# Scores of chunks 3 to 5 on 64x64 tiles of TensorE, four heads a matmul

## The chip, the cores and the metric

The kernel runs on one core of a Trainium2 chip. The metric is the device time of one execution in microseconds (us), as the median of several runs. TensorE (PE in the profile, with PEld for its weight loads) multiplies matrices, VectorE (DVE), ScalarE (ACT) and GpSimd (POOL) work elementwise, and SyncE (SP) issues nearly all DMAs.

## What is computed

The reference is a state-space attention block (Mamba-2, SSD) followed by an MLP with hard-swish. `x` is 4 batches x 8 heads x 768 tokens x 32, `B` and `C` have a state size of 16, and `a` is a decay of each token.

```python
log_a = np.log(np.clip(a, 1e-06, 1.0))
for c in range(nc):                                   # chunks of the sequence
    cum = np.cumsum(la, axis=-1)
    L = np.exp(cum[:, :, :, None] - cum[:, :, None, :]) * causal
    CB = np.einsum('bhin,bhjn->bhij', Cc, Bc)         # the scores
    y_intra = np.einsum('bhij,bhjd->bhid', CB * L, xc)
    y_inter = np.einsum('bhin,bhnd->bhid', Cc, state) * np.exp(cum)[:, :, :, None]
    y[:, :, sl] = y_intra + y_inter
    state = decay_full[:, :, None, None] * state + np.sum(Bx, axis=2)
# heads side by side: 3072 tokens x 256
h = x @ w_in                                          # 256 -> 2048
g = h * np.clip(h + 3.0, 0.0, 6.0) / 6.0
return (g @ w_out).astype(np.float32)                 # 2048 -> 256
```

The result of the recurrence does not depend on the chunk's length; the kernel uses chunks of its own.

## The kernel before

The kernel cuts the 768 tokens into `NC` = 6 chunks of 128, each split into two halves of 64 tokens. Chunk by chunk it does the attention part for all 4 batches and 8 heads, and then the MLP for the 512 tokens (4 batches x 128) of that chunk. The order of instructions is written out by hand: the attention work of chunk c = k + 1 is woven into the MLP of block k, and each engine takes its instructions in that order.

**One MLP block.** For k >= 1, the loop `for f in range(2, NF)` (L1084) is the first product, with 16 slices of 128 hidden units. Slice f's result `h` lies in one of six banks of PSUM (f0 to f3, y0, y1, in turn). `squares` (L696) starts the slice f, `cross` (L713) ends slice f - 2, `enlarge` (L704) scales the bank between them (on VectorE where f % 4 is 3, else on ScalarE), and `factor` does ramp and product of hard-swish: ScalarE writes `gT` from `h` (L730), VectorE multiplies it by `h` in place (L735). GpSimd makes sums of `gT` (`g_sums`, L784, its operations at L796) for the second product, at f = 6, 10, 14 and after the loop. Then `wide_units` (L865), a generator of 14 units, does the second product (matmuls at L874). It collects the output in two tiles, `wide` and `back`: VectorE transposes `wide` into `back` in blocks of 32x32 (`turned_back`, L882), and SP stores `back` in 32 DMAs of 16 KB. The last block has `out_units` (L798) in its place. In block 0, `first_out` (L738) writes the output through the same two buffers.

**The scores.** For chunk c, `bTs[c]` holds three tiles with state sizes and heads on the partitions (8 heads x 16 = 128) and tokens along the free dimension: `bT` from B, `csT` from C, and `cT`, two copies of C's transpose. Copy t of `cT` is zero except for the heads whose number is t modulo 2; `parity` (128x2) holds the zeros and ones for it. `scores` (L516) makes, for each batch b, half a and pair of heads q, one matmul on a tile of 32 rows x 64 columns: the 32 partitions of the pair from `bT` against those of both copies of `cT`, 2 x 64 = 128 columns, into the bank f{q}. That is 32 matmuls a chunk. `multiply` (L562) then multiplies the decays `L` by the scores on VectorE, one operation for each bank (L574), and `mix` (L604) multiplies the result by x.

**Where that stands.** The transposes of chunk `ahead` = k + 2 are made by `turn_all` (L483): for chunk 2 at the end of block 1's first product, for chunks 3 to 5 in unit 9 of block k's second product (L1141), on VectorE: two 32x32 transposes (L465), the two copies of `cT` (`part_heads`, L475) and `fade` (L481), which multiplies `csT` in place by decays for the products with the state. The scores of chunk c = 3, 4, 5 stand behind unit 2 of the second product of block k = c - 1 (L1124). For chunks 3 and 4, `own_banks` (L508) puts the products with the state (`from_state`, L503, tiles of 32x64) directly ahead of the scores; for chunk 5 they come one unit earlier (L1122). `into_state` (L544, tiles of 64x32) follows the scores.

`TURN` is 2. Chunks 0 and 1 are transposed in other ways, and chunk 2's copies are made on ScalarE.

Of the kernel before, what the change touches and what calls it, by code (L numbers as in the profile page):

```python
# [21 lines left out]
def kernel(  # L22
# [24 lines left out]
    nc = tc.nc  # L47
# [107 lines left out]
    def conceal_in(t, pattern):  # L155
# [27 lines left out]
        out=head, in_=head, pattern=[[2 * N, NQ], [N, 2]], compare_op=ALU.is_ge,  # L183
        fill=0.0, base=N - 1, channel_multiplier=-1)
    parity = const.tile([P, 2], FP32, name="parity")

    def decode(i):

# [211 lines left out]
    def carry(c):  # L400
# [3 lines left out]
            out=tmps[c], in0=states[c - 1],  # L404
            in1=etos[c][:, :, HT - 1:HT].to_broadcast([P, NB, 2 * D]), op=ALU.mult)

    def turned(c):
        if c not in bTs:
            bTs[c] = [att.tile([P, NB, P], FP32, name="bT", bufs=1),
                      att.tile([P, NB, 2, P], FP32, name="cT", bufs=1),  # L410
                      att.tile([P, NB, P], FP32, name="csT", bufs=1)]
        return bTs[c]

# [49 lines left out]
    def turn_squares(t, out):  # L463
# [2 lines left out]
            out=out.rearrange("r b (s a) -> r b a s", a=4),  # L466
            in_=t.rearrange("s t b a n -> s (b a) t n"))

    def part_heads(c):
        _, cT, csT = turned(c)  # L470
        for t in range(2):
            if c == TURN:
                nc.scalar.activation(cT[:, :, t], csT, AF.Copy, scale=parity[:, t:t + 1])
            else:
                nc.vector.tensor_scalar(  # L475
                    out=cT[:, :, t], in0=csT, scalar1=parity[:, t:t + 1], scalar2=None,
                    op0=ALU.mult)
# [5 lines left out]
    def turn_all(c):  # L483
        bT, _, csT = turned(c)
        for t, out_ in zip(bcs[c], (csT, bT)):
            turn_squares(t, out_)
        part_heads(c)
        fade(c)

    def busy(n, bank):  # L490

# [24 lines left out]
    def scores(c):  # L516

        bT, cT, _ = bTs[c]
        cbs[c] = [ps.tile([P, NB, 2, HT], FP32, name="cb", tag=f"f{q}") for q in range(NQ)]
        if c not in ys:
            own_banks(c)
        for b in range(NB):
            for a, rows in enumerate(HALF):
                for q in range(NQ):
                    pair = slice(32 * q, 32 * q + 32)
                    nc.tensor.matmul(  # L530
                        out=cbs[c][q][rows, b], lhsT=bT[pair, b, rows],
                        rhs=cT[pair, b, :, rows], start=(b == 0), stop=True,
                        tile_position=(32 * q, a * HT), skip_group_check=True)
        if c == TURN:
            from_state(c, 0)
        into_state(c, *range(2 if c not in (TURN, NC - 1) else 1))
# [25 lines left out]
    def multiply(c):  # L562

        if c < NC - 1 and c != TURN:
            take(c)
        mids[c] = mid = att.tile([P, NB, 2 * D], FP32, name="mid", bufs=1)
        if c == 0:
            for t in range(2):
                nc.scalar.activation(
                    mid[:, :, t * D:(t + 1) * D], sps[c][0][:, :, t * D:(t + 1) * D], AF.Copy,  # L570
                    scale=parity[:, t:t + 1])
        for q in (2, 0, 1, 3) if c in (TURN, NC - 1) else range(NQ):
            hs = slice(2 * q, 2 * q + 2)
            nc.vector.tensor_tensor(  # L574
                out=Ls[c][:, :, hs], in0=Ls[c][:, :, hs], in1=cbs[c][q], op=ALU.mult)
            if c and c != TURN and q == 1:
                new_state(mid, sps[c][0], tmps[c])

# [137 lines left out]
    def factor(k, f):  # L716
        ramp(k, f, hs_[k, f])
        times_ramp(k, f, hs_[k, f])
# [19 lines left out]
    def first_out(b, i, c):  # L738

        if i == 0 and b % 2 == 0:
            outs[b // 2] = ps_o.tile([P, 2, DM], FP32, name="o", tag="o")
        o = outs[b // 2]
        for f in range(i * FP, (i + 1) * FP):
            if b == NB - 1 and f >= NF - 2:
                lead(c, f - NF + 2)
            nc.tensor.matmul(  # L748
                out=o[:, b % 2], lhsT=gTs[0][:, f, b * P:(b + 1) * P], rhs=w_out[:, f],
                start=(f == 0 and b % 2 == 0), stop=True, skip_group_check=True)  # L750
        if i == NP - 1 and b % 2:
            ob = ffn.tile([P, 4, DM], FP32, name="ob", tag=("wide", "back")[b // 2])[:, :2]
            nc.scalar.copy(out=ob, in_=o)
            nc.sync.dma_start(
                out=out.rearrange("(b s) m -> s b m", b=NB)[:P, b - 1:b + 1], in_=ob)
# [42 lines left out]
    def out_units(k):  # L798


        def quarter(e, r, t):
            return g_quarter(k, e, r)[:, :, t * P:(t + 1) * P]

        def total(n, t):
            return gsums[k][n][:, :, t * P:(t + 1) * P]

        def unit(bank, slot, lhs, rhs, js=range(NJ), clear=False):

            for j in js:
                nc.tensor.matmul(  # L810
                    out=bank[:, slot], lhsT=lhs[:, j], rhs=rhs[:, j],
                    start=(clear and j == 0), stop=True, skip_group_check=True)

        for t in range(2):
            oa = ps_o.tile([P, 4, P], FP32, name="oa", tag="o")
            if t == 0:

                most, rest = range(NJ - 1), range(NJ - 1, NJ)
                unit(oa, 0, quarter(0, 0, 0), w4[:, 0, 0], most, clear=True)
                yield  # L820
                unit(oa, 3, quarter(0, 0, 1), w4[:, 0, 0], most)
                yield
            unit(oa, 1, quarter(1, 0, t), w4[:, 1, 0], clear=(t == 1))
            if t == 0:
                unit(oa, 0, quarter(0, 0, 0), w4[:, 0, 0], rest)
                unit(oa, 3, quarter(0, 0, 1), w4[:, 0, 0], rest)
                x1 = ffn.tile([P, 2, P], FP32, name="x1", tag="third")
                nc.scalar.copy(out=x1, in_=oa[:, 0:4:3])
            yield
            ob = ps_o.tile([P, 4, P], FP32, name="ob", tag="o")  # L830
            unit(ob, 3 - 3 * t, quarter(1, 1, t), wsums[4], clear=True)
            yield
            unit(oa, 2, total(2, t), wsums[2])
            res = ffn.tile([P, 8, P], FP32, name="res", tag=("wide", "back")[t])
            nc.vector.tensor_tensor(
                out=res[:, 0:5:4], in0=oa[:, 1:3],
                in1=x1[:, t:t + 1].to_broadcast([P, 2, P]), op=ALU.add)
            yield
            unit(ob, 2, total(4, t), w4[:, 1, 1])
            yield  # L840
            unit(ob, 3 * t, total(1, t), wsums[1])
            u = ffn.tile([P, 2, P], FP32, name="u", tag="u2")
            u2 = res[:, 4:5].to_broadcast([P, 2, P])
            if t:
                nc.vector.tensor_tensor(out=u, in0=ob[:, 0:4:3], in1=u2, op=ALU.add)
                nc.vector.tensor_tensor(out=res[:, 1], in0=ob[:, 2], in1=u[:, 1], op=ALU.add)
            yield
            if t:

                unit(oa, 0, quarter(0, 1, t), wsums[3], clear=True)  # L850
                nc.vector.tensor_tensor(
                    out=res[:, 2:4], in0=oa[:, 0:1].to_broadcast([P, 2, P]), in1=u, op=ALU.add)
            else:
                unit(ob, 1, quarter(0, 1, t), wsums[3])
                nc.vector.tensor_tensor(out=u, in0=ob[:, 0:2], in1=u2, op=ALU.add)
                nc.vector.tensor_tensor(out=res[:, 1:3], in0=ob[:, 2:4], in1=u, op=ALU.add)
                nc.vector.tensor_tensor(out=res[:, 3], in0=ob[:, 0], in1=u[:, 1], op=ALU.add)
            for r in range(2):
                r0 = (t + 2 * r) * S + k * P
                nc.sync.dma_start(  # L860
                    out=out[r0:r0 + P, :],
                    in_=res[:, 2 * r:2 * r + 2].rearrange("p m c -> p (m c)"))
            yield

    def wide_units(k):  # L865
# [10 lines left out]
                    start=(clear and j == 0), stop=True, skip_group_check=True)  # L876

        near, far = range(NJ // 2), range(NJ // 2, NJ)
        res = ffn.tile([P, 2, 2, 2 * P], FP32, name="wide")
        back = ffn.tile([P, 2, TB], FP32, name="back")  # L880

        def turned_back(m, r=None):  # L882

# [27 lines left out]
        yield  # L911
        product(oc, 0, w4[:, 1, 0], halves[1][0], far)
        product(oa, 0, w4[:, 0, 0], halves[0][0], far[-1:])
        nc.scalar.copy(out=res[:, 0, 0], in_=oc[:, 0])
        nc.vector.tensor_tensor(out=res[:, 0, 0], in0=oa[:, 0], in1=res[:, 0, 0], op=ALU.add)
        yield
# [103 lines left out]
    load_eto(1)  # L1020
    load_bc(1)
    load_x(1)


    weave, g_done = {}, {}
# [4 lines left out]
    for k in range(NC):  # L1030
# [53 lines left out]
        for f in range(2, NF):  # L1084
# [7 lines left out]
            cross(k, f - 2)  # L1092
            enlarge(k, f)
            factor(k, f - 2)
            if f in ((8, 12) if k == 1 else (3, 7)) and ahead < NC:
                conceal(ahead, int(f in (7, 12)))
            if f == NF - 1 and k not in gsums:
# [78 lines left out]
```

## Time and profile before

| | |
|---|---|
| median of 3 runs | 343.59 us (343.59 to 344.37) |
| the profiled execution | 343.4 us, of which the span of its instructions is 341.7 |
| TensorE busy | 333.8 us, 3372 matmul records |
| VectorE, ScalarE, GpSimd busy | 210.7, 188.3, 145.4 us |
| scores, L530 | 384 records, 7.4 us busy, a record 277 ns on average |
| copies of cT on VectorE, L475 | 8 operations, 4.2 us |
| granted clock of TensorE | 1.00 |

The profile shows one execution. A row names the line, the engine, the operation and the tiles it writes and reads, with the number of instructions, their busy time and the mean of one. Matmul records overlap each other, so the busy time of a group is less than the number times the mean. The chain of waits follows the work that ended last back to the start: what stands in it set the time. The time of a run is that of the whole launch and is a little longer than the span.

### The profile page before, as it was taken

What the parts mean: (1) busy time and instruction counts of PE and PEld (TensorE: products, weight loads), DVE (VectorE), ACT (ScalarE), POOL (GpSimd) and SP (SyncE); (2) the same over time, 40 slices, a digit from 0 to 9 for tenths busy, and PEclk for the clock granted to TensorE, in tenths of its full rate; (3) what the DMA queues carried; (4) which work ended last, traced back from release to release, by engine and by line L of the source; (5) the groups of instructions that cost most, each with busy time, mean ns of one, the idle gap of its engine ahead of it and who ended that gap; (6) DMA issues with size and microseconds to landing.
All of it is one profiled execution on the core that took longest, in us unless ns stands there. A gap on an engine that the chain in (4) does not pass through costs nothing.

```text
span 341.7 us, 8203 instructions
## 1 busy us (share of the span) xinstructions
PE 333.8 (98%) x3372; PEld 267.5 (78%) x3372; DVE 210.7 (62%) x332; ACT 188.3 (55%) x394; POOL 145.4 (43%) x139
## 2 busy tenths in 40 slices
PE   5999999999999999999999999999999999999996
PEld 2554448888878888888888888888888888888996
DVE  6699999996499739665519465528465323465011
ACT  4778878667987481675471676470576030576000
POOL 3300000381282998099803089810089600079600
PEclk9999999999999999999999999999999999999999
DMA  8989967052690216167107294001260001110000
GB/s 172 174 312 197 209 233 153 2 59 69 164 114 8 58 55 119 25 84 70 24 27 144 33 96 62 16 2 18 33 75 2 2 4 17 30 17 2 0 33 31
DMA packets 89605, 25.15 MB, mean 74 GB/s; under 512 B 82208, under 2 KB 85952, under 8 KB 89056
## 3 DMA queue, kind: packets, MB, share of 16 engines
q1 hardware_dynamic: 85184, 23.33, 36.5%
q10 hardware_dynamic: 4384, 1.31, 1.8%
q8 instruction: 26, 0.43, 0.5%
q14 instruction: 11, 0.09, 0.1%
HBM read 21.33 MB, written 3.29 MB: 72 GB/s over the span
## 4 chain that ended last, share of the span: by engine, by line
PE 94%; DMA 3%; DVE 1%; SPq 1%; issue 0%; DVEq 0%
PE h L692 33%; PE wb L874 13%; PE wc L874 8%; PE o L748 8%; PE h L626 8%; PE wa L874 8%; PE oa L810 4%; PE ob L810 4%; PE y L604 3%; PE y L503 2%; PE cb L530 2%; DMA raw<-in_moe_w_in_dram 2%; PE y L544 1%; DMA pairs<-in_C_dram 1%; SPq L101 1%; DVE L L574 0%
## 5 line engine op out<-in xcount | busy, mean ns | idle before, releaser
L735 DVE SCALAR_TENSOR_TENSOR gT<-gT,h 128x512 f32<-128x512 f32 x96 | 64.9, 686 | 41.1 <-ACT gT L730 39.9
L730 ACT ACTIVATE gT<-h,half 128x512 f32<-128x512 f32 x96 | 65.2, 684 | 17.8 <-PE h L692 15.9
L796 POOL TENSOR_TENSOR s<-gT 128x512 f32<-128x512 f32 x20 | 28.9, 1443 | 76.2 <-DVE gT L735 76.1
L711 ACT ACTIVATE h<-h 128x512 f32<-128x512 f32 x62 | 35.8, 583 | 43.6 <-PE h L692 39.3
L692 PE MATMUL h<-y_hi,w_part 128*128 128x512 f32 x160 | 51.8, 409 | 0.0
L692 PE MATMUL h<-y_less,w_part 128*128 128x512 f32 x160 | 49.7, 397 | 0.0
L692 PE MATMUL h<-y_lo,w_part 128*128 128x512 f32 x160 | 49.5, 395 | 0.0
L692 PEld LDWEIGHTS h<-y_lo,w_part 128*128 128x128 f32 x160 | 30.0, 188 | 7.4
L692 PEld LDWEIGHTS h<-y_less,w_part 128*128 128x128 f32 x160 | 30.0, 188 | 6.9
L692 PEld LDWEIGHTS h<-y_hi,w_part 128*128 128x128 f32 x160 | 30.0, 188 | 6.8 <-DVE gT L735 0.4
L385 ACT ACTIVATE L<-L,cum_n 128x64 f32<-128x64 f32 x128 | 31.6, 338 | 0.0
L874 PE MATMUL wb<-s,w_out 128*128 128x256 f32 x128 | 30.6, 382 | 0.0
L748 PE MATMUL o<-w_out,gT 128*128 128x256 f32 x128 | 28.8, 381 | 0.0
L626 PE MATMUL h<-yT,w_in 128*128 128x512 f32 x64 | 27.7, 594 | 0.0
L748 PEld LDWEIGHTS o<-w_out,gT 128*128 128x128 f32 x128 | 24.1, 190 | 3.8 <-issue 0.5
L403 POOL TENSOR_TENSOR tmp<-state,eto 128x256 f32<-128x256 f32 x5 | 3.4, 673 | 55.3 <-ACT eto L389 55.2
L874 PEld LDWEIGHTS wb<-s,w_out 128*128 128x128 f32 x128 | 24.0, 190 | 3.6
L796 POOL TENSOR_TENSOR s<-gT,s 128x512 f32<-128x512 f32 x20 | 26.0, 1306 | 1.3
L796 POOL TENSOR_TENSOR gT<-gT 128x512 f32<-128x512 f32 x20 | 25.7, 1291 | 1.3
L796 POOL TENSOR_TENSOR s<-s,gT 128x512 f32<-128x512 f32 x20 | 25.7, 1290 | 0.0
L158 POOL TENSOR_SCALAR_AFFINE_SELECT L<-L 64x1024 f32<-64x1024 f32 (+1 forms) x16 | 20.4, 1280 | 10.5 <-DMA L<-cum_d 10.1
L396 POOL TENSOR_TENSOR bs<-B,L 128x128 f32<-128x128 f32 x24 | 12.7, 545 | 26.0 <-ACT L L385 20.9
(138 smaller groups left out, 507.5 us busy)
## 6 DMA issues: line engine op xcount, KB each, us to landing
raw<-in_moe_w_out_dram SPq DMA_DIRECT2D x4, 1024.0 KB
L<-cum_d SPq DMA_DIRECT2D x8, 512.0 KB
xt<-in_x_dram SPq DMA_DIRECT2D x6, 512.0 KB
raw<-in_moe_w_in_dram SPq DMA_DIRECT2D x3, 1024.0 KB
out_dram<-back SPq DMA_DIRECT2D x128, 16.0 KB
pairs<-in_C_dram SPq DMA_DIRECT2D x40, 32.0 KB
eto<-cum_e SPq DMA_DIRECT2D x20, 64.0 KB
B<-in_B_dram SPq DMA_DIRECT2D x5, 256.0 KB
```

Of the source, the lines that this page charges most:

```text
L158: nc.gpsimd.affine_select(out=t[rows], in_=t[rows], pattern=pattern, compare_op=ALU.is_ge, fill=-1e5, base=base, channel_multiplier=-1)
L385: nc.scalar.activation(Ls[c][:, b, h], Ls[c][:, b, h], AF.Exp, bias=cum_n[:, c, g:g + 1])
L396: nc.gpsimd.tensor_tensor(out=bss[c][:, hs], in0=Bs[c][:, hs], in1=Ls[c][:, b, :, HT - 1:HT].to_broadcast([P, NH, N]), op=ALU.mult)
L626: nc.tensor.matmul(out=h, lhsT=w_in[f // FP][:, j, f % FP * P:(f % FP + 1) * P], rhs=yTs[k][:, j].rearrange("p b i -> p (b i)"), start=(j ...
L692: nc.tensor.matmul(out=hs_[k, f], lhsT=w[j][:, f % FP * P:(f % FP + 1) * P], rhs=y[:, j], start=(start and j == 0), stop=True, skip_group_ ...
L711: nc.scalar.activation(h, h, AF.Copy, scale=1.0 / EPS + 1.0)
L730: nc.scalar.activation(gTs[k][:, f], h, AF.Relu, bias=half, scale=1.0 / 6.0)
L735: nc.vector.scalar_tensor_tensor(out=g, in0=g, scalar=1.0, in1=h, op0=ALU.min, op1=ALU.mult)
L748: nc.tensor.matmul(out=o[:, b % 2], lhsT=gTs[0][:, f, b * P:(b + 1) * P], rhs=w_out[:, f], start=(f == 0 and b % 2 == 0), stop=True, skip_ ...
L796: nc.gpsimd.tensor_tensor(out=o, in0=p_, in1=q_, op=op)
L810: nc.tensor.matmul(out=bank[:, slot], lhsT=lhs[:, j], rhs=rhs[:, j], start=(clear and j == 0), stop=True, skip_group_check=True)
L874: nc.tensor.matmul(out=bank[:, slot], lhsT=lhs[:, j], rhs=rhs[:, j], start=(clear and j == 0), stop=True, skip_group_check=True)
```

## The change

For chunks 3, 4 and 5 the scores are made on tiles of 64 rows x 64 columns. A matmul takes four heads: their 64 partitions from `bT` against those of four copies of C's transpose, 4 x 64 = 256 columns. That is 16 matmuls a chunk. Copy t of the four is zero except for the heads whose number is t modulo 4; the new constant `fourth` (128x4) holds the zeros and ones. The banks now hold two batches and four heads each, in place of four batches and two heads, and `multiply` reads them so.

The four copies are not made in `turn_all` with the transposes. They are made by `part_fours` on VectorE, one in each of the iterations f = 11 to 14 of the first product of block k = c - 1, and `fade` follows in f = 15.

`cT` has moved from the pool `att` into the buffer of the output's staging: `wide` and `back`, and their counterparts in the first and the last block, become the two halves of one tile, and `cT` shares its buffer. In `wide_units` that tile is taken in unit 5, after the scores.

```diff
+    fourth = const.tile([P, NQ], FP32, name="fourth")
...
+    def heads_apart(n):
+        return ffn.tile([P, NB, n, P], FP32, name="cT", tag="wide")
+
+    def both_halves(name):
+        return ffn.tile([P, 2, 2, TB], FP32, name=name, tag="wide")
...
             bTs[c] = [att.tile([P, NB, P], FP32, name="bT", bufs=1),
-                      att.tile([P, NB, 2, P], FP32, name="cT", bufs=1),
+                      heads_apart(2) if c <= TURN else None,
                       att.tile([P, NB, P], FP32, name="csT", bufs=1)]
...
+    def part_fours(c, ts):
+        if 0 in ts:
+            bTs[c][1] = heads_apart(NQ)
+        _, cT, csT = bTs[c]
+        for t in ts:
+            nc.vector.tensor_scalar(
+                out=cT[:, :, t], in0=csT, scalar1=fourth[:, t:t + 1], scalar2=None, op0=ALU.mult)
...
-        part_heads(c)
-        fade(c)
+        if c == TURN:
+            part_heads(c)
+            fade(c)
...
-        cbs[c] = [ps.tile([P, NB, 2, HT], FP32, name="cb", tag=f"f{q}") for q in range(NQ)]
+        shape = [P, NB, 2, HT] if c <= TURN else [P, NB // 2, NQ, HT]
+        cbs[c] = [ps.tile(shape, FP32, name="cb", tag=f"f{q}") for q in range(NQ)]
...
-                for q in range(NQ):
+                for q in range(NQ if c <= TURN else 0):
                     pair = slice(32 * q, 32 * q + 32)
...
+                for r, four in enumerate(HALF if c > TURN else ()):
+                    nc.tensor.matmul(
+                        out=cbs[c][2 * r + b // 2][rows, b % 2], lhsT=bT[four, b, rows],
+                        rhs=cT[four, b, :, rows], start=(b % 2 == 0), stop=True,
+                        tile_position=(r * HT, a * HT), skip_group_check=True)
...
-            hs = slice(2 * q, 2 * q + 2)
-            nc.vector.tensor_tensor(
-                out=Ls[c][:, :, hs], in0=Ls[c][:, :, hs], in1=cbs[c][q], op=ALU.mult)
+            if c <= TURN:
+                part = Ls[c][:, :, 2 * q:2 * q + 2]
+            else:
+                part = Ls[c][:, 2 * (q % 2):2 * (q % 2) + 2, HU * (q // 2):HU * (q // 2) + HU]
+            nc.vector.tensor_tensor(out=part, in0=part, in1=cbs[c][q], op=ALU.mult)
...
-        res = ffn.tile([P, 2, 2, 2 * P], FP32, name="wide")
-        back = ffn.tile([P, 2, TB], FP32, name="back")
+        res, back = None, None
...
         product(oa, 0, w4[:, 0, 0], halves[0][0], far[-1:])
+        both = both_halves("wide")
+        res, back = both[:, 0].rearrange("p m (r i) -> p m r i", r=2), both[:, 1]
...
+    nc.gpsimd.tensor_tensor(
+        out=fourth.rearrange("p (q t) -> p q t", q=2), in0=head[:, :2], in1=head[:, 2:],
+        op=ALU.add)
...
             factor(k, f - 2)
+            if TURN < c < NC and f > 10:
+                if f < 15:
+                    part_fours(c, (f - 11,))
+                else:
+                    fade(c)
```

## The prediction, made before the changed kernel had run

> **What bounds the kernel now.** I read the page first, then the chain of waits in order of time, then the rows of the lines that the diff touches, and last VectorE and GpSimd in the stretch into which work moves.
>
> ```profile
> span 341.7 us, 8203 instructions
> PE 333.8 (98%) x3372; PEld 267.5 (78%) x3372; DVE 210.7 (62%) x332; ACT 188.3 (55%) x394; POOL 145.4 (43%) x139
> ...
> PE 94%; DMA 3%; DVE 1%; SPq 1%; issue 0%; DVEq 0%
> ```
>
> TensorE is busy for 98% of the span and is 94% of the chain that ended last. So whatever lengthens or shortens TensorE's own work after the start-up is paid in full, and what happens on the other engines counts only where TensorE has to wait for it. The chain, in order of time, around the scores of chunk 3 and of chunk 5 (start, length, what, number of records):
>
> ```profile
> 163.65 0.55 PE y L503 x25
> 164.19 0.01 PE cb L530
> 164.20 0.01 PE y L503
> 164.21 0.04 PE cb L530 x2
> 164.25 0.02 PE y L503 x3
> 164.27 0.98 PE cb L530 x55
> 165.25 0.79 PE y L544 x53
> 166.04 1.92 PE wb L874 x8
> ...
> 265.07 0.62 PE y L503 x32
> 265.70 1.92 PE wb L874 x8
> 267.62 1.14 PE cb L530 x63
> 268.76 0.58 PE y L544 x32
> ```
>
> No wait stands between these pieces: TensorE goes from one to the next. A float32 matmul of the program is two records in the trace, so a chunk's 32 score matmuls are 64 records. In chunk 3 (chunk 4 looks the same, at 215.41) the products with the state and the scores run into each other and take 165.25 - 163.65 = 1.60 us; in chunk 5 the scores stand alone and take 1.14 us. All six chunks' scores are 7.4 us of busy time; the change can touch some 4 us of the kernel directly.
>
> **The change, part by part.**
>
> *Columns through the array.* This is the term that decides. Before, a score matmul occupies a tile of 32 rows by 64 columns and streams 128 columns of C; eight such tiles fit the array, so 64 records are 8 rounds of 8. Now a matmul occupies 64x64, of which four fit, and streams 256 columns: 16 matmuls, 32 records, again 8 rounds, but each of twice the columns. Price of a round: a record over the whole array with 256 columns takes 1.73 / 8 = 0.216 us (wb L874, 8 records in 1.73), one with 128 columns 1.79 / 16 = 0.112 us (oa L810). That tiles run side by side at this rate is seen in the products with the state: 32 records of 64 columns on four tiles take 0.62 us, which is 8 rounds of 0.054 (a quarter of 0.216) and 0.19 left for entering a new tile shape; single records confirm it, as rounds start 58 to 59 ns apart. The old scores show rounds 109 ns apart while they run undisturbed. So the new scores are 8 x 0.216 = 1.73 us of columns, and the 0.19 for the entry (wb shows the same: 1.92 for 8 records behind small tiles, 1.73 otherwise): 1.92 us.
>
> Chunk 5: 1.92 - 1.14 = **+0.78 us**. Chunks 3 and 4: the scores follow the products with the state, which use 32x64 tiles. Before, both have one shape and overlap; now the shape changes between them and each stands alone, 0.62 + 1.92 = 2.54 against 1.60, **+0.94 us** each. The sum is 0.78 + 2 x 0.94 = +2.66 us. No row of before has a float32 matmul on 64x64 tiles, so I bound it: at the low end the entry and the change of shape cost nothing, 1.73 - 1.14 = 0.59 each, +1.8; at the high end the old scores' own excess over their columns (1.14 - 8 x 0.108 = 0.28) takes the place of 0.19, +2.9. I take +2.66, as two rows give the 0.19.
>
> *Fewer records and weight loads.* 32 loads fewer a chunk. Weight loads overlap (PEld is a row of its own), and the 0.216 us of a round is more than the 0.131 us of a load, so nothing is left to gain beyond what the columns already give. By the Trainium skill, TensorEngine Tiling (Array Packing), Instruction Overhead, each matmul has about 60 cycles of overhead on trn2, which speaks for this change; at the 2.4 GHz that the Trainium skill, TensorE: Matmul & The Clock Gate, Part 1, states, an estimate of 0.8 us a chunk for 32 records in a row, which would cancel the columns. The rounds above, 109 ns for eight records of 128 columns, have no room for it.
>
> *VectorE's work, moved.* The two masked copies (TENSOR_SCALAR cT, median 460 ns) and the fade (L481, 693 ns) leave the late part of the block before; nothing on TensorE waited for them there, so nothing is won. Four copies, one each in f = 11 to 14 of the first product, and the fade in f = 15, are added: 4 x 0.46 + 0.69 = 2.5 us. VectorE is busy for 12.3 of the 19.9 us of that loop in each of the three blocks, so by busy time it fits: an iteration is 1.39 us, and VectorE's gated product takes 0.69 of it, plus 0.69 where it also scales h (f = 11 and 15). If it alone counted, the last copy would push f = 15's scaling (157.99 to 158.68) by some 0.6 us; its user is the pair of h records at 160.16, 1.48 us later. I cost it at nothing; the cover is that 1.48 us.
>
> *The port shared with GpSimd.* GpSimd runs its sums without a break through f = 11 to 15 (153.18 to 168.8 in this block). The trace has one place where these copies met a long GpSimd operation, at 134 us:
>
> ```profile
> 134.12 1.46 POOL L158 TENSOR_SCALAR_AFFINE_SELECT L<-L 128x1024 f32<-128x1024 f32 x1
> 134.17 1.70 DVE L475 TENSOR_SCALAR cT<-csT,parity 128x512 f32<-128x512 f32 x2
> ```
> ```profile
> L475 DVE TENSOR_SCALAR cT<-csT,parity x8: 397/460/1366, 14.2 to 236.1; 128x512 f32<-128x512 f32 x8
> ```
>
> The first copy took 397 ns and GpSimd's operation, at best 1148, took 1463; the second copy took 1366 and ended 0.28 us after GpSimd's. They exclude each other and alternate. Each of the four copies may thus wait for a sum to end (1.2 to 1.3 us). I followed the queue: with copies of 0.28 us between sums of 1.22, the copies in chunk 3's block end at 154.75, 156.2, 157.65 and 159.15, and f = 15's scaling at 159.8, against the 160.16 at which TensorE needs it. Chunk 4's comes out at 211.6 against 211.92, and chunk 5's at 262.4 or 263.6 against 263.32, depending on whether its first copy gets in before the sum at 256.95. So the margin shrinks to about 0.3 us but holds in most cases: I take 0, and keep up to 1 us a block for the range. The Trainium skill, SBUF — State Buffer, Who interferes with whom, calls the pair an exclusive lock and counts an operation with two SBUF inputs in, so the fade too; the trace agrees (y_lo, 683 ns alone, 1757 beside sums).
>
> *Waits and memory.* cT now lies where the output of the previous block is staged, so the first copy waits until the last of 32 stores, issued at 148.98, has landed (150.5 by the DMA records); the copy comes at about 153.9. Blocks 3 and 4 have more (199.2 against 205.6, 250.3 against 257.0). The staging tile in turn waits for the scores, which TensorE does 3 units earlier. The banks: the scores now take f0 and f2 first, and f3 in their second half, later than before. VectorE's product with L keeps its four operations of 682 ns; its first can start when half of the scores are done, and its reader (L604 at 173.70) comes 5 us after it ends. GpSimd's one small added operation at about 25 us, under 0.6 us by its nearest rows, has slack until chunk 1's state. SP issues the same DMAs in the same order. All at 0.
>
> Sum: the profiled execution took 343.4 us (span 341.7 and 1.7 around it); + 2.66 gives 346.1. The median of the runs is 343.59, 0.2 above; the forecast for the time is **346.2 us**.
>
> **The rivals.**
> 1. *VectorE comes late.* The copies and the fade alternate with GpSimd's sums, and TensorE waits for f = 15's scaling, or in chunk 5, where the products with the state stand one unit earlier (265.07), for the fade. For it: the 1366 ns and margins of 0.3 us. Against it: all three margins come out just positive, and the fade is due 2 us later. Price 0.3 to 1.0 us a block on top of the forecast: 347 to 349.2.
> 2. *Two tiles at a time instead of four.* The two records of a float32 matmul follow each other on one tile; if that blocked the queue, rounds would hold two: 1.73 us more a chunk, +5.2 on the forecast, 351.4. The state products' rounds of four 58 ns apart speak against it.
> 3. *The other side: records, not columns, set the time.* If the scores' 1.14 us were the price of 64 records (17.8 ns each), 32 would take 0.57: -0.57 in each of three chunks, 341.9. In its favour, the later records of the old scores start about 16.7 ns apart rather than 13.6. It decides only if four 64x64 tiles get through 256 columns in less than 0.14 us (1.14 / 8), where every row shows 0.216. This is where the page's fixed overhead would lead, halfway: columns and records cancel, no change.
> 4. *Nothing measurable.* Entry and shape change cost nothing, and the new scores overlap with their neighbours as the old ones did: +1.0 or less.
>
> **How the numbers follow.** Forecast (+1.8 to +2.9, no waits) 0.68; rival 1 0.18; rival 2 0.04; rival 3 0.03; rival 4 0.07. A measurement of this kernel tells about 0.3% (1.0 us) from no change. Faster by more 0.03, within 0.06, slower by more 0.91, the forecast and rivals 1 and 2 and a little of rival 4. The range runs from 345.2 (below the low bound, 343.6 + 1.8, by the part of rival 4 next to it) to 348.0 (the high bound, 346.5, and rival 1 with half its price).
>
> **What would show it.** Right: TensorE's rows for cb have 192 records of 64x64 tiles beside 192 old ones, the chain shows about 1.9 us for them in chunks 3 to 5, and the products with the state before them keep 0.62. Rival 1 would show as idle time of TensorE before h L692 or y L503, released by VectorE, and copies of over 1 us. Rival 2: cb of 3.5 us. Rival 3: cb below 1.1 us. I am wrong if cb is near 1.9 us and the span has not grown by about 2.5: then a piece I hold to be paid in full was covered.

## The result and the profile after

The changed kernel took **348.06 us** in the median of 6 runs (346.61 to 350.61), beside 343.6 us for the kernel before (6 runs, 343.45 to 344.37): a ratio of 1.0134 [1.0093, 1.0174], with the 95% interval in brackets. Ratios leave out an execution over 1.5% above the fastest of its kernel, which is one in all, of 352.22 us. The changed kernel is slower, as forecast, but by some 4.5 us where 2.6 were forecast, and the median lies just above the range. The runs of the changed kernel spread over 4 us, those of the kernel before over 0.9; three of the six show a mean granted clock of 0.995 (348.27, 349.45, 350.61 us), the other three 1.0 (347.18 us on average). The profiled execution is the fastest of the six, 346.61 us with a span of 344.9, so it shows 3.2 us of the growth.

The page of the changed kernel, its head and its chain by engine:

```profile
span 344.9 us, 8035 instructions
...
PE 335.5 (97%) x3276; PEld 268.3 (78%) x3276; DVE 218.7 (63%) x338; ACT 188.3 (55%) x394; POOL 147.7 (43%) x140
...
PE 93%; DVE 3%; DMA 1%; ACT 1%; issue 1%
```

TensorE has 96 matmul records and 96 weight loads fewer, and is busy 1.7 us longer. New in the chain is "issue 1%": time in which TensorE waited for nothing that the profile shows. The larger shares of DVE and ACT come from block 1's first product (90 to 100 us), where the chain leads through their work though TensorE waits only 0.22 us; the kernel before with an unused constant (below), in which no work has moved, has the same piece of chain. The chain of waits around chunk 3 and chunk 5 (start, length, what, number of records):

```profile
158.66 1.73 PE wa L902 x8
160.38 0.46 PE h L716 x2
...
163.86 0.62 PE y L519 x32
164.49 1.89 PE cb L552 x32
166.38 0.79 PE y L566 x53
...
266.48 0.62 PE y L519 x32
267.11 1.92 PE wb L902 x8
269.03 1.89 PE cb L552 x32
```

Products with the state and scores now stand apart, 166.38 - 163.86 = 2.52 us against 1.60 before. The new scores take 1.89 us a chunk, in chunk 5 against 1.14. And further on in the same chain, after chunk 5's sums (`mix`, L628) and chunk 5's last products with the state:

```profile
279.04 1.41 PE y L628 x90
280.45 0.62 PE y L519 x32
281.07 1.27 issue
282.35 1.89 PE wb L902 x8
```

In the kernel before the same three pieces follow each other without the wait:

```profile
276.88 1.41 PE y L604 x90
278.29 0.62 PE y L503 x32
278.91 1.92 PE wb L874 x8
```

The chain's pieces, added up, account for the span:

| piece of TensorE's chain | before | after | difference | forecast |
|---|---|---|---|---|
| chunk 3, products with the state and scores | 1.60 | 2.52 | +0.92 | +0.94 |
| chunk 4, the same | 1.60 | 2.51 | +0.91 | +0.94 |
| chunk 5, scores | 1.14 | 1.89 | +0.75 | +0.78 |
| "issue" at 281 us | 0 | 1.27 | +1.27 | 0 |
| "issue" at 20 us | 0.17 | 1.04 | +0.87 | 0 |
| start-up, up to the first scores | 15.20 | 14.64 | -0.56 | 0 |
| four loops of the first product, 86 records each | 19.95 each | 19.79 each | -0.66 | 0 |
| wc, twice (shorter entry) | 3.58 | 3.45 | -0.26 | 0 |
| sum of these | | | +3.24 | +2.66 |

The span grew by 3.19 us; pieces under 0.3 us make up the rest. So the term that I had worked out, +2.66, is there to 0.08 us. What I had not seen is a wait of TensorE of 1.27 us, and a gain of 0.16 us in each loop that the diff doesn't touch.

VectorE's new work, in the block before chunk 3 and before chunk 5 (timelines of VectorE: start, length):

```profile
158.50 0.91 DVE L481 TENSOR_SCALAR cT<-csT,fourth 128x512 f32<-128x512 f32 x1
159.33 0.69 DVE L732 TENSOR_SCALAR h<-h 128x512 f32<-128x512 f32 x1
```
```profile
264.29 1.79 DVE L496 TENSOR_TENSOR csT<-csT,eto 128x512 f32<-128x512 f32 x1
```

The last copy ends at 159.41, the scaling of f = 15 at 160.02, and TensorE's pair of h records follows its predecessor at 160.38 without a gap. The fade, which takes 0.68 us before chunks 3 and 4, takes 1.79 before chunk 5, and ends at 266.08, 0.4 us before its reader at 266.48. TensorE does not wait, but the margins are 0.4 us.

### The profile page after: what moved, and what is told of

It reads as the page before. It is cut to its first block, busy times and chain, and to the rows that moved or that the text cites. A ratio compares the mean times of both kernels' runs of the same rounds, so it can differ in the third digit from the quotient of the medians.

```text
span 344.9 us, 8035 instructions
## 1 busy us (share of the span) xinstructions
PE 335.5 (97%) x3276; PEld 268.3 (78%) x3276; DVE 218.7 (63%) x338; ACT 188.3 (55%) x394; POOL 147.7 (43%) x140
## 4 chain that ended last, share of the span: by engine, by line
PE 93%; DVE 3%; DMA 1%; ACT 1%; issue 1%
PE h L716 29%; PE wb L902 12%; PE wc L902 8%; PE o L772 8%; PE h L650 8%; PE wa L902 8%; PE oa L836 4%; PE ob L836 4%; PE y L628 3%; PE y L519 2%; PE cb L552 2%; PE y L566 1%; PE cb L547 1%; DMA pre<-in_a_dram 1%; PE d L509 1%
## 5 line engine op out<-in xcount | busy, mean ns | idle before, releaser
L822 POOL TENSOR_TENSOR gT<-gT 128x512 f32<-128x512 f32 x20 | 26.8, 1346 | 1.3
L650 PEld LDWEIGHTS h<-yT,w_in 128*128 128x128 f32 x64 | 12.1, 190 | 14.9 <-issue 12.9
```

Of the source, the lines that this page charges most:

```text
L650: nc.tensor.matmul(out=h, lhsT=w_in[f // FP][:, j, f % FP * P:(f % FP + 1) * P], rhs=yTs[k][:, j].rearrange("p b i -> p (b i)"), start=(j ...
L822: nc.gpsimd.tensor_tensor(out=o, in0=p_, in1=q_, op=op)
```

## What the wait is

The trace has a DMA queue that carries instructions, q8 (a second, q14, has 11 packets in both kernels). The page's row (packets, MB, share of the engines' time), before and then after:

```profile
q8 instruction: 26, 0.43, 0.5%
```
```profile
q8 instruction: 25, 0.41, 0.5%
```

Its packets are 16 KB each. TensorE has 6744 loads and matmuls before and 6552 after, about 260 for each packet; the compiled program has 64 bytes for an instruction, so that 16 KB hold 256. The chains of the ten profiled executions of this study hold 13 waits of over 0.3 us put down to "issue". All 13 end 1.33 to 1.60 us after the end of such a packet. Seven places, the kernel before's short wait among them (us; the kernels with 64 instructions more and with quarters are described below):

```
kernel, place                    the packet      TensorE goes on   after its end
before, at 20 us                 17.85 to 18.86      20.30            1.44
after, at 20 us                  18.41 to 19.31      20.70            1.39
after, chunk 5                  279.98 to 280.97    282.35            1.38
after once more, chunk 5        280.48 to 281.47    282.83            1.36
before + 64, chunk 1             79.67 to 80.54      82.04            1.50
before + 64, chunk 5            279.73 to 281.01    282.44            1.43
before, quarters, chunk 0        24.54 to 25.49      26.83            1.34
```

A count shows that they are TensorE's program. With TensorE's loads and matmuls counted in the trace from its start, the 13 waits stand at five places only: behind 700 (in every kernel that waits at 20 us), 955, 1972 to 1974, 5801 and 6056 of them. In the compiled programs, which hold a few other instructions in between, these are the places 708, 964, 1988, 5828 and 6084, and they differ by whole multiples of 256. So TensorE waits at borders of blocks of 256 in its own program. Borders of this spacing number 26 in the kernel before and 25 after, as many as the packets; taken in order, the packet that ends ahead of each wait is the one for the block behind that border.

By the same count TensorE enters the block ahead of the wait at 279.23 in `after`, within the sums of chunk 5. The next packet starts 0.75 us later, takes 1.0, and TensorE goes on 1.4 after it: some 3.1 us in which TensorE lives on the block that it has. A block lasts longer than that nearly everywhere: wb's eight records with their eight loads keep TensorE 1.73 us, so 256 instructions of that kind last 28 us. But the 128 records of the sums on tiles of 64x32, with their 128 loads, are 256 instructions in 1.41 us. Whether they meet a border badly depends on where the borders fall.

A short block alone is not enough. In the kernel before, the block from 163.69 to 165.55, chunk 3's products with the state, its scores and the first of `into_state`, lasts 1.9 us, and TensorE does not wait behind it: the next packet had started at 160.53, 3.2 us before TensorE entered the block, while long matmuls ran. In that trace, behind the start-up, packets start 0.6 to 1.3 us after TensorE enters a block in the midst of small matmuls, and up to about 4 us ahead of it elsewhere.

The change takes 16 matmuls, of two loads and two records each, from each of three chunks: 3 x 64 = 192 instructions, which moves all later borders by 192, or, as borders come every 256, by 64 the other way.

**The theory**: the growth beyond the tiles is a wait for TensorE's own instructions, made by the position of the borders and not by any work. **The rivals**: the copies and the fade moved on VectorE (or their shift in memory) cost the rest somewhere out of the profiled execution's sight; or the new tiles cost more than the rows show. A further question was whether the spread of the runs is the same wait at different lengths.

## The experiments

Each kernel ran 6 times or more; the first four shared runs of the kernel before (median 343.83 us, 343.27 to 345.58), the last four others (343.73, 343.12 to 345.9). The ratios are made from runs side by side, so that they are not quite the quotients of the medians.

### The changed kernel once more

No edit.

> The changed kernel once more, unchanged, for a second profile and the spread of its times (346.6 to 350.6 us so far, where the kernel before keeps within 1 us). Theory 1 (code): TensorE's instructions come in transfers of 16 KB, 256 instructions each; where such a block lies wholly in small matmuls it is used up before the next has landed, and TensorE waits, as it did for 1.27 us at 281 us. Then this profile shows a wait at the same instruction, of another length, and the median is again near 348. Theory 2 (port): VectorE's copies wait for GpSimd's sums, and the slower runs are those where TensorE waits in the first product's end for f = 15. Then this profile has idle time before h or y, released by VectorE, and none of over 1 us behind y L519 in chunk 5.

347.06 us in the median of five executions (345.88 to 348.78; a sixth took 352.22, and with it the median is 347.86), ratio 1.0081 [1.005, 1.0113]. The interval meets the first one's only between 1.0093 and 1.0113. This time the profiled execution is one with a mean clock of 0.995. Its chain at the same place:

```profile
278.81 1.41 PE y L628 x90
280.22 0.62 PE y L519 x32
280.84 1.99 issue
282.83 3.57 PE wb L902 x8
```

The same instruction waits, 1.99 us in place of 1.27, and then eight records of wb take 3.57 us instead of 1.89. The table of stretches of this kernel says why wb was slower (stretch, length, busy time and number on TensorE, its loads, VectorE, ScalarE and GpSimd, then the granted clock, the DMA share and GB/s):

```profile
279.00:280.80 1.80, 1.80 (x156) 1.64 (x134) 0.00 (x0) 0.74 (x2) 0.00 (x0) 1.00 0.03 9
282.80:286.20 3.40, 3.37 (x9) 2.65 (x9) 2.13 (x4) 0.00 (x0) 0.00 (x0) 0.51 0.06 10
287.00:290.00 3.00, 3.00 (x16) 2.64 (x15) 0.00 (x0) 0.11 (x1) 0.00 (x0) 1.00 0.18 27
```

The granted clock is half for 3.41 us from 282.87 on, which loses 1.7 us of work, and 1.7 of 347 is the missing 0.005 of the mean clock. The longer wait itself comes from a later packet: by the count above, TensorE entered the block at 279.01 and the packet started at 280.48, 1.47 us later instead of 0.75. So the wait costs twice: 1.3 to 2.0 us directly, and 1.7 more when it is long enough for the clock to fall. The runs at 0.995 without a profile fit this, but their waits were not seen. A mean clock of 0.995 also stands beside 3 of the 46 executions of the kernel before that the experiments share, and 3 of 12 with the old tiles (below), which have no wait in chunk 5; so the clock alone does not tell the place. The Trainium skill, TensorE: Matmul & The Clock Gate, HAM oscillation, warns of idle gaps of more than about 3.4 us; here 1.99 us, behind 2 us of small matmuls, were enough, and 1.27 us were not, nor were 1.66 us at the same place in the kernel before with 64 more.

### The changed kernel with 128 more instructions on TensorE

In block 0's first product each of the 32 matmuls is cut into two of 256 columns. The work is the same, the borders move by 128.

```diff
         for j in range(NK):
-            nc.tensor.matmul(
-                out=h, lhsT=w_in[f // FP][:, j, f % FP * P:(f % FP + 1) * P],
-                rhs=yTs[k][:, j].rearrange("p b i -> p (b i)"),
-                start=(j == 0), stop=(j == NK - 1))
+            for cs in (slice(0, TB // 2), slice(TB // 2, TB)) if True else (slice(0, TB),):
+                nc.tensor.matmul(
+                    out=h[:, cs], lhsT=w_in[f // FP][:, j, f % FP * P:(f % FP + 1) * P],
+                    rhs=yTs[k][:, j].rearrange("p b i -> p (b i)")[:, cs],
+                    start=(j == 0 and cs.start == 0), stop=True, skip_group_check=True)
```

> The changed kernel, with each of the 32 matmuls of block 0's first product cut into two of half the columns: the same result, 128 more instructions on TensorE ahead of chunk 1, so that all later block borders of the code stand 128 instructions earlier in the work. The halves cost under 0.3 us. Theory 1: by the order of instructions, no block of 256 lies wholly in small matmuls any more; no wait at 281 us, span 343.6 to 344.2, median near 345.7, spread under 1.5 us. Theory 2: as the changed kernel, near 348 with a spread of 4.

346.09 us (345.87 to 347.08), ratio 1.0057 [1.0038, 1.0077]. The chain has no wait behind the sums of chunk 5 any more (products with the state end at 281.60, wb starts there), and the runs lie within 1.2 us. With more instructions the median is 1.0 us below that of the repetition beside it (347.06) and 2.0 below the first one (348.06). The two ratios' intervals overlap, so the medians alone show the gain weakly; that the wait is gone, the chain shows. Small waits remain, 0.69 us at 19.9 and 0.32 at 80.2.

### The kernel before with 64 more

The same cut in 16 of the 32 matmuls (f below 8). The tiles, the copies and the memory are those of before; only the borders stand as the change would put them for chunk 5.

```diff
+            for cs in (slice(0, TB // 2), slice(TB // 2, TB)) if f < 8 else (slice(0, TB),):
```

> The kernel before, with 16 matmuls of block 0's first product cut in two: 64 more instructions on TensorE, work otherwise as before, under 0.2 us for the halves. Theory 1: a block of code now lies in the scores, products with the state and sums of chunk 4, at about 217 us, and TensorE waits there: +0.7 to +2 us, and a wider spread than before. Theory 2 and any other that has the loss in the new tiles or in VectorE: 343.6 to 343.9, spread under 1 us.

347.04 us (346.06 to 349.86), ratio 1.0094 [1.0062, 1.0126], with nothing added but 16 cuts. The chain of this kernel, in chunk 1 and in chunk 5:

```profile
80.25 0.65 PE y L503 x26
80.90 1.13 issue
...
280.16 0.62 PE y L503 x32
280.78 1.66 issue
282.44 1.99 PE wb L875 x8
```

The wait stands behind the same products as in the changed kernel. My expectation had it near 217 us: I had moved the borders in the wrong direction. The kind of effect and its size were as the theory had them, the place was not. This kernel also pays a second wait, in chunk 1, which the change doesn't have, since its 192 instructions are missing only from chunk 3 on. The two waits, 2.8 us together, are most of the 3.2 by which its median grew.

### Everything but the tiles

Copies, fade, memory and `fourth` as in the changed kernel; the scores stay on 32x64 tiles and read the two of the four copies that hold their heads.

```diff
-                for q in range(NQ if c <= TURN else 0):
+                for q in range(NQ):
...
-                        rhs=cT[pair, b, :, rows], start=(b == 0), stop=True,
+                        rhs=cT[pair, b, (2 * (q % 2) if c > TURN else 0):(2 * (q % 2) if c > TURN else 0) + 2, rows],
+                        start=(b == 0), stop=True,
...
-                for r, four in enumerate(HALF if c > TURN else ()):
+                for r, four in enumerate(()):
```

The banks and `multiply` are put back to their old form in the same way.

> All of the change but the tiles: the four masked copies, their place in the first product, the fade and the new memory, with the old scores of 32 rows by 64 columns and 128 columns, which read the two copies of the four that they need. TensorE has the instructions of the kernel before. Theory of the sum: the tiles were the loss, so no more than the kernel before; and if the shorter loops of the first product (19.79 against 19.95 us) come from the new place of the memory, 0.5 us less: 343.1. Theory 2: VectorE's moved work costs here too, 345 or more.

343.44 us (342.66 to 345.17), ratio 0.999 [0.9973, 1.0007]. What the change does on VectorE, GpSimd and in memory costs nothing that the runs can tell; that rival has fallen. The number of TensorE's instructions is that of before, and the chain has no wait in chunk 5, only one of 1.09 us at 20 us. The changed kernel with 128 more has border waits of the same sum, 0.69 + 0.32 = 1.01 us. The difference of these two is 346.09 - 343.44 = 2.65 us by the medians, and 2.3 us by the two ratios (1.0057 and 0.999): the tiles.

### The kernel before with 128 more

The same cut in all 32 matmuls.

> The kernel before with all 32 matmuls of block 0's first product cut in two: 128 more instructions on TensorE ahead of chunk 1, twice those of the run with 64 more. Theory of code: the wait depends on where the block borders fall, not on how many instructions were added; no wait of over 0.5 us after 25 us, median 343.8 to 344.4. Rival (cutting the matmuls is what costs): +6 us, twice the loss with 64 more.

344.1 us (343.41 to 345.39), ratio 1.0013 [0.9998, 1.0027]. Twice the cuts of the kernel with 64 more cost 0.4 us, which the interval does not tell from nothing, where those cost 3.2: it is the position that costs, not the number of instructions or the cutting. Its chain has no "issue" above 0.2 us. If the 0.4 us are the cuts' price, which the changed kernel with 128 more pays too, the tiles cost 0.4 less than the difference above: 1.9 to 2.65 us in all.

### The kernel before with memory moved by 32 and by 64 bytes

For the shorter loops there were two candidates: VectorE's work was moved, or the constant `fourth` moves every tile behind it in SBUF by 32 bytes. An unused constant does the second alone.

```diff
     parity = const.tile([P, 2], FP32, name="parity")
+    const.tile([P, 4], FP32, name="unused")
```

> The kernel before with one constant of 128x4 added that nothing reads, in the place of the change's: the tiles behind it lie 32 bytes later, and w_part, y_lo and y_less begin at a multiple of 64 bytes instead of half of one. Theory of the place: the loops of the first product (h, 86 records) take 19.79 us instead of 19.95, and the median falls by 0.5 to 0.7 us. Rival (the loops are shorter because VectorE's work was moved): 19.95 and no change.

343.23 us (342.33 to 346.44), ratio 0.9991 [0.997, 1.0012], which alone tells nothing. The chain's row for a loop does, by the same 86 records: first the changed kernel, then this one.

```profile
191.21 19.79 PE h L716 x86
```
```profile
190.61 19.79 PE h L693 x86
```

All four loops take 19.79 us, against 19.95 and 19.96 before, so the gain comes from the place of the tiles in memory; the medians can't tell it. With 64 bytes (`[P, 16]` in place of `[P, 4]`):

> The same with a constant of 128x16, which moves the tiles by 64 bytes, so that they begin at half of 64 bytes as in the kernel before. Theory of the place, by the 64 bytes: loops of 19.95 us and the time of the kernel before. If any movement helps: 19.79.

343.34 us (342.7 to 344.07), ratio 0.9982 [0.9966, 0.9997], and loops between the two:

```profile
191.03 19.87 PE h L693 x86
```

My idea that the tiles must begin at a multiple of 64 bytes does not explain a value in between. Which rule of the address it is stays open.

### A try for a better version

The kernel before with 32 bytes more, and with the masks at the start (`diff_mask`, `diff_less`, which add up the decays' differences) cut into four matmuls of 128 columns, to move the first border away from the sums at 20 us:

```diff
+    def in_quarters(o, lhsT, rhs, start):
+        for h in range(0, NH, 2):
+            nc.tensor.matmul(
+                out=o[:, h:h + 2], lhsT=lhsT, rhs=rhs[:, h:h + 2],
+                start=(start and h == 0), stop=True, skip_group_check=True)
...
+        in_quarters(d, ident_h, hide.unsqueeze(1).to_broadcast([P, NH, HT]), True)
```

> A try for a version that beats both: the kernel before with the constant of 128x4 that nothing reads, and with the masks and the first products of the decays at the start (L336, L343, L348) cut into four matmuls of 128 columns, 108 more instructions on TensorE ahead of chunk 0's scores. Theory of code: the block border that makes TensorE wait at 20 us (0.2 to 1.1 us in the runs so far) moves out of the chunk's small matmuls, and none of the later borders lies badly; with the shorter loops, 342.3 to 343.2. If the wait at 20 us comes from something else, 343.2 to 343.6 and a wait of 0.2 us or more at the sums of chunk 0.

349.74 us (349.48 to 351.79), ratio 1.0185 [1.0161, 1.021]: the worst of all. The chain, and the wait's stretch in the table of stretches (columns as above):

```profile
21.13 0.67 PE y L606 x46
21.80 5.02 issue
26.83 0.46 PE y L606 x13
```
```profile
22.00:26.80 4.80, 0.00 (x0) 0.00 (x0) 2.14 (x4) 0.00 (x0) 0.00 (x0) 0.95 0.88 338
```

A border fell into chunk 0's sums while the DMA engines were busy for 0.88 of the time at 338 GB/s. By the count, TensorE had entered the block before at 19.70, and the packet started only at 24.54. TensorE waited 5.02 us, and then had half the clock for 6.8 us. In the kernel before, the same packet also starts 4.0 us after the border, at 24.29; there the block also holds some 25 long matmuls of the first product and lasts 13 us, so nothing waits. No kernel of this study is clearly faster than the kernel before.

## Why the prediction was wrong

**The sum for the tiles was right.** +2.66 was forecast; the profile has +2.58, and the experiments have 1.9 to 2.65. The rounds of four tiles with 256 columns start 0.216 us apart, as records of 256 columns over the whole array do; the scores took 1.89 of the 1.92 us, and the products ahead of them kept 0.62. Rivals 2 (3.5 us a chunk) and 3 (below 1.1) are refuted by that row, and so is rival 4, as the tiles alone cost 1.9 us or more. The sign that I gave, 192 new records, was a miscount: three chunks of 32 are 96, and the trace has 96.

**VectorE and the shared port were right.** The copies alternate with GpSimd's sums (906 to 1093 ns each before chunks 3 and 4, against 397 to 486 undisturbed; 480 to 619 before chunk 5) and end within 0.4 us of the times worked out (155.11, 156.55, 157.98 and 159.41 for 154.75, 156.2, 157.65 and 159.15), and the loop starts 0.37 us later than in the kernel before. The scaling ends at 160.02, 0.36 us before TensorE wants it. Rival 1 was not paid. The fade met a sum in chunk 5 and took 1.79 us, as the row of y_lo had it (1757 ns), still 0.4 us early. The Trainium skill, SBUF — State Buffer, Who interferes with whom, and the trace agree here, now for the fade as well.

**The step that failed** is "*Fewer records and weight loads*", with its verdict that "nothing is left to gain". I priced an instruction only by the time that it holds the array. It also holds a place in TensorE's program, which comes in blocks of about 256, and 192 places fewer put a border where the small matmuls of chunk 5's sums use a block up before the next has come. That wait is 1.27 and 1.99 us in the two profiled executions, in the second with 1.7 us more by the halved clock. From the runs, the changed kernel stands 348.06 - 346.09 = 2.0 us (1.0 in the repetition) above its version with 128 instructions more, whose cuts may themselves cost 0.4: so the borders cost 1.0 to 2.4 us in the median. The medians grew by 4.5 us and, in the repetition, by 3.2 (347.06 against 343.83). That tiles, borders and memory add up to this is no check, since each is a difference of neighbouring medians; the check is the chain, where tiles and wait stand apart as rows of their own. Which side of the range's upper end, 348.0, a median falls on is chance, as 348.06 and 347.06 show; the wait is in both profiles.

The list of waits that I costed at 0 was a list of semaphores, buffers and queues; a wait that no semaphore shows wasn't in it, and no rival had it. The sign that could have told me stands in the trace of before: a wait of 0.17 us, put down to "issue", in the sums at 20 us, where the border was almost met. The Trainium skill, Runtime: NRT & Kernel Launch, Instruction fetch mechanics, has blocks of 16 KiB or 256 instructions, as the packets here, and calls the cost of crossing a border mostly hidden; that holds for nearly all of the 25 to 27 borders of each kernel here, and fails by up to 5.0 us at some that fall into small matmuls.

The waits at 20 us differ from run to run (1.04 and 0.55 in the two profiles of the same kernel, 0.17 before) and stand ahead of all instructions that the change removes. In the profiled execution a start-up shorter by 0.56 us cancels most of the longer wait. I put neither down to the change.

What stays open: what sets the start of a packet, which comes 0.75 and 1.47 us after TensorE has entered the block before it in the two profiles of the changed kernel, and up to about 4 us ahead of that where long matmuls run. It is also open why the wait at 20 us differs between executions of one kernel; all kernels but the changed one have one profile. That the spread of the changed kernel's other runs is this wait and the clock behind it is argued from their mean clock and from the narrow spread without the wait (1.2 us), not seen.

## What to carry to other kernels

A change in the number of an engine's instructions moves the borders of its instruction blocks for all that follows, so where TensorE runs stretches of 200 and more tiny matmuls, such a change can win or lose 1 to 3 us, and in one case here 6, that belong to no work; look for "issue" in the chain, compare it with the ends of the instruction queue's packets, and test with a version that has 64 or 128 instructions more. Before a version with fewer instructions is rejected or kept, it is worth trying at another position: here 1 to 2 us went away by cutting 32 matmuls in two. Fewer, larger matmuls on larger tiles gain nothing if each streams as many more columns as there are fewer of them and fewer tiles fit the array: count rounds times columns, and add the entry of a new tile shape.

## What the runs showed of the hardware that I had not expected

- From the end of an instruction packet to TensorE's next instruction 1.33 to 1.60 us pass, wherever TensorE waited for it. Blocks entered out of small matmuls that lasted 3.1 to 3.8 us, the wait included, made it wait 1.1 to 2.0 us; one of 1.9 us, entered out of long ones, did not.
- The places where TensorE waited lie whole multiples of 256 instructions apart, in all kernels.
- After a wait of 1.99 us behind small matmuls the clock was half for 3.41 us; after 5.02 us, for 6.83 us; after 1.27 and 1.66 us, not at all.
- A shift by 32 bytes of all tiles behind one constant made 86 float32 records with 512 columns faster by 0.8% (19.95 to 19.79 us), one by 64 bytes by 0.4%.
